# One written order for all engines from the last output product on, token transposes moved to TensorE, and conditional weight splits in smaller blocks

## The chip, the cores and the metric

The kernel runs on one core of a Trainium2 chip. The engines are TensorE (PE, with its weight loads shown apart as PEld), VectorE (DVE), ScalarE (ACT), GpSimd (POOL) and SyncE (SP, which here only issues DMAs). The metric is the device time of one execution in microseconds (us); a kernel's time is the median of its runs. Times within the kernel come from one profiled execution.

## The reference

Three layers follow each other. The queries, keys and values are 4 x 8 x 576 x 64 (batch, heads, sequence, head size); the attention is causal by blocks of 64.

```python
attn = softmax(mask(q @ k.T / sqrt(64))); x = attn @ v        # -> 2304 tokens x 512
xn = x / rms(x) * rms_g
x = (silu(xn @ w_gate) * (xn @ w_val)) @ w_out                # 512 -> 1536 -> 512
logits = normed(x) @ normed(expert_emb).T / tau               # 8 experts, tau = 0.1
e = argmax(logits); gate_w = softmax(logits)[e]
out = gate_w * (relu(x @ w1[e]) @ w2[e])                      # 512 -> 1024 -> 512, one expert a token
```

Which expert a token gets is found at run time, so the kernel routes: it sorts the tokens by expert in a table in DRAM, gathers 128 tokens of one expert at a time, and scatters the results to their rows.

## The kernel before, in words

**Tiles.** The 2304 tokens are nine units `u` of 256 tokens (`NU` = 9, the last is `NU-1`), each in two halves `j` of 128. For accuracy, most operands are a sum of two 16-bit parts, hi and lo, and a product is made as hi x hi + hi x lo + lo x hi, three matmuls where one would do.

**First layer of a unit.** `gate_mm` (L530) makes the gate product `g` and the value product `v` for one of six pieces `s` of the 1536 hidden columns: 2 x 24 products of 128 x 256 for `g` and the same for `v`. ACT takes the tanh (`gate_t`, L541), DVE combines (`gate_a`, L547 and L549), ACT writes the hi part of `hT` and POOL the lo part (`gate_b`, L554 and L555). `out_mm` (L567) then makes the output product of one half `j`, 36 products of 128 x 512, six for each piece of `hT`. `out_ev` (L578 to L591) brings the result into `R`, 128 tokens as hi and lo, one buffer. `R` is written to DRAM (`x2s`), and SP starts a DMA transpose of it into `x2T` (L590), from which PE makes the routing logits (`route_a`, L608). For the second half of the last unit, PE transposes `R` itself (L1103), and DVE copies the result out of the accumulator bank (L1104).

**Routing.** `route_b` to `route_d` find the expert of each token, its gate weight and its place, and POOL scatters rows into the table `tbl` (L672). While the last unit is still computed, `fullest` (L816 on) picks the two experts with most tokens so far and gathers the first table rows of the fullest into `tb2`; `fullest_ids` (L846) transposes `tb2` on PE (L849), DVE copies out the token numbers, POOL gathers the tokens of the first two steps (`xg`, L747), SP transposes them by DMA into `xt` (L749), and the expert's weights are loaded in four quarters a layer (`raw`, L722) and split into hi by ACT (`whi`, L727) and lo by DVE (`wlo`, L728).

**Expert steps.** There are 20 steps of 128 tokens: `mm1` (L764) is the first product, `ev1` the relu, `mm2` (L788) the second product, `ev2` the scaling and the scatter into the output (L796). Steps 0 and 1 use the expert found early. While they run, `T` counts the tokens of each expert; DVE makes `nbc`, the number of blocks (L1114 and L1115), a small product with `nbc` gives the order of all other steps (L1119), and POOL fetches the token numbers of steps 2 and 3 (L1127) and their tokens (L747 again). From step 2 on a step that has another expert than the step before loads new weights: `next_w` (L732 to L737) puts the split of a layer's four quarters into one conditional block on ACT and DVE.

**Order.** Up to the last output product the Tile scheduler orders the work, by priorities that the program sets (`step`) and by what is ready in its model. From `manual_schedule()` on (L1075) each engine runs its instructions as the program writes them. Before the change, that call stands behind the last output product; `seq` lists what stands ahead of it. Every engine runs its own queue in order, so a waiting instruction holds all behind it.

Of the kernel before, what the change touches and what calls it, by code (L numbers as in the profile page):

```python
# [8 lines left out]
F32 = mybir.dt.float32  # L9
F16 = mybir.dt.float16  # L10
# [8 lines left out]
P = 128  # L19
# [12 lines left out]
def attention_moe_moe(ctx: ExitStack, tc: tile.TileContext, q, k, v, w_gate, w_val, w_out, rms_g, emb, tau, w1, w2, out):  # L32
# [540 lines left out]
    def out_ev(u, j):  # L573
# [12 lines left out]
        if (u, j) == (NU - 1, 1):  # L586
            nc.scalar.dma_start(out=x2s[r0:r0 + P, :], in_=R)
            fl['R'] = R
            return
# [135 lines left out]
    def split_w(l, behind=()):  # L725
        for c in range(NC):
# [5 lines left out]
    def next_w(l, i):  # L732
# [3 lines left out]
        with tc.If(ch > 0):  # L736
            split_w(l)  # L737
# [4 lines left out]
    def gather(i, ids=None, last=UNIT):  # L742
# [5 lines left out]
        xt = xt_b[i % 3]  # L748
        tr = nc.sync.dma_start_transpose(out=xt, in_=xg)  # L749
        fl[f"xg{i}"], fl[f"xt{i}"] = ld.ins.name, tr.ins.name  # L750
        xgT[i] = xt
# [93 lines left out]

    def fullest_ids():  # L846
        t2 = ps_g.tile([P, 3, 2], F32, tag="o", name="t2", bufs=2)
        for c in range(3):
            tr = nc.tensor.transpose(t2[:, c, :], fl["tb"][0:2, :, c], idn[0:2, 0:2])  # L849
            tc.add_manual_dep(tr.ins, marks[-1], NOSYNC, reason="not before this product")  # L850
# [3 lines left out]
        for z in range(2):  # L854
            gather(z, id2[:, z:z + 1])
        fl["ev"] = [nc.values_load(em_i[0:1, z:z + 1], engines=[ENG.SP], min_val=0, max_val=NE - 1,
                                   skip_runtime_bounds_check_because="made on the chip in this range") for z in range(2)]
        for l in range(2):
            preload(0, l, ('no', 'tb_in')[l])
            split_w(l, ('gate_t', 'gate_a'))  # L860
# [108 lines left out]
    def step(kind, u, s):  # L969
        tc.cur_priority += PRI  # L970
        if kind == "gate":
# [5 lines left out]
            if u == NU - 1 and s == FS:  # L977
                fullest_ids()
# [6 lines left out]
        else:  # L985
            out_mm(u, s)
            if u == NU - 1 and s == 0:
                preload(1, 0, None)
            out_ev(u, s)
            if u == NU - 1 and s == 0:  # L990
                preload(1, 1, "x2T")
# [9 lines left out]
        if kind == "out" and s == 0 and u == NU - 1:  # L1001
            route(u, [0])
        if kind == "out" and s == 1 and u < NU - 1:
# [67 lines left out]
    seq += [("out", NU - 1, 0), ("out", NU - 1, 1)]  # L1071
# [3 lines left out]
    ctx.enter_context(tc.manual_schedule())  # L1075
    fin = late[0].tile([P, 16], F32, name="fin")
# [22 lines left out]
    u, js = NU - 1, [1]  # L1099
    mm1(0, range(3), behind=fl['out'])  # L1100
    xp = ps_g.tile([P, 2 * KD, P], F16, tag="o", name="xp", bufs=2)
    for c in range(2 * KD):
# [139 lines left out]
```

## Time and profile before

| what | value |
|---|---|
| median of 3 runs | 868.64 us (865.67 to 872.69) |
| the profiled execution | 876.56 us |
| its span on the chip | 874.8 us |
| its mean granted TensorE clock | 0.967 |
| PE busy | 795.9 us, 91% |
| DVE, ACT, POOL busy | 461.2, 450.0, 356.0 us |
| mean DMA rate | 154 GB/s |

The attention and most of the first layer fill the span up to about 600 us. The change starts in the last unit of the first layer, and the first expert products run at about 635 us. A timeline gives the start and the duration of an instruction, or of several alike in a row (`x24`), and in brackets how long its engine stood idle before it and what ended the wait. [...]

### The profile page before, as it was taken

What the parts mean: (1) busy time and instruction counts of PE and PEld (TensorE: products, weight loads), DVE (VectorE), ACT (ScalarE), POOL (GpSimd) and SP (SyncE); (2) the same over time, 40 slices, a digit from 0 to 9 for tenths busy, and PEclk for the clock granted to TensorE, in tenths of its full rate; (3) what the DMA queues carried; (4) which work ended last, traced back from release to release, by engine and by line L of the source; (5) the groups of instructions that cost most, each with busy time, mean ns of one, the idle gap of its engine ahead of it and who ended that gap; (6) DMA issues with size and microseconds to landing.
All of it is one profiled execution on the core that took longest, in us unless ns stands there. A gap on an engine that the chain in (4) does not pass through costs nothing. (4 is left out here: it accounts for less than half of the span.)

```text
span 874.8 us, 21909 instructions
## 1 busy us (share of the span) xinstructions
PE 795.9 (91%) x8574; PEld 602.6 (69%) x8574; DVE 461.2 (53%) x981; ACT 450.0 (51%) x929; POOL 356.0 (41%) x362
## 2 busy tenths in 40 slices
PE   2679799879999999989999999999988999999994
PEld 2579477757667777767777777758576777667771
DVE  6999978635355435355545454225542275462352
ACT  6978776845455656555746442212411274462351
POOL 5556466756533656543746322222323121202110
PEclk9989889989999999999999999999999999999997
DMA  8565899885777676687785351114755499998794
GB/s 240 163 191 141 182 246 208 163 152 100 123 151 139 117 137 113 119 159 140 133 134 104 64 105 23 28 45 113 226 158 124 85 291 298 208 320 190 181 238 128
DMA packets 296637, 135.11 MB, mean 154 GB/s; under 512 B 249852, under 2 KB 280743, under 8 KB 296522
## 3 DMA queue, kind: packets, MB, share of 16 engines
q1 hardware_dynamic: 288650, 117.00, 62.5%
q0 software_dynamic: 4080, 10.56, 4.3%
q10 hardware_dynamic: 3792, 6.03, 2.1%
q8 instruction: 70, 1.15, 0.6%
q14 instruction: 45, 0.37, 0.1%
HBM read 129.30 MB, written 10.25 MB: 160 GB/s over the span
## 5 line engine op out<-in xcount | busy, mean ns | idle before, releaser
L530 PE MATMUL g<-xT,wg 128*128 128x256 f16 x1296 | 158.5, 277 | 1.7 <-DMA xT<-hl 1.7
L530 PE MATMUL v<-xT,wv 128*128 128x256 f16 x1296 | 158.6, 277 | 0.0
L567 PE MATMUL o<-wo,hT 128*128 128x512 f16 x648 | 152.6, 384 | 3.2 <-ACT o L580 3.2
L530 PEld LDWEIGHTS <-wg 128*128 128x128 f16 x1296 | 126.7, 100 | 25.3 <-issue 2.0
L530 PEld LDWEIGHTS <-wv 128*128 128x128 f16 x1296 | 125.1, 99 | 16.3
L764 PE MATMUL h<-xt,whi 128*128 128x128 f16 x1280 | 112.1, 220 | 4.5 <-DMA xt<-xg 3.5
L764 PE MATMUL h<-xt,wlo 128*128 128x128 f16 x640 | 110.0, 220 | 0.7 <-issue 0.5
L567 PEld LDWEIGHTS <-hT 128*128 128x128 f16 x648 | 61.2, 98 | 67.8 <-issue 5.2
L764 PEld LDWEIGHTS <-whi 128*128 128x128 f16 x1280 | 99.9, 98 | 10.6 <-issue 6.2
L728 DVE SCALAR_TENSOR_TENSOR wlo<-raw,whi 128x1024 f16<-128x1024 f32 x64 | 76.7, 1236 | 48.0 <-ACT whi L727 43.4
L788 PE MATMUL o<-whi,hl 128*128 128x512 f16 x320 | 96.4, 383 | 2.4 <-issue 2.4
L555 POOL TENSOR_TENSOR hT<-h,hT 128x512 f16<-128x512 f32 x54 | 63.7, 1179 | 73.6 <-ACT hT L554 71.9
L417 POOL TENSOR_TENSOR pl<-pf,ph 128x512 f16<-128x512 f32 x66 | 69.6, 1076 | 52.7 <-issue 45.7
L788 PEld LDWEIGHTS <-hl 128*128 128x128 f16 x480 | 46.5, 99 | 57.1 <-issue 6.6
L727 ACT ACTIVATE whi<-raw 128x1024 f16<-128x1024 f32 x64 | 65.2, 1051 | 39.9 <-DMA raw<-in_moe_w_dram 29.2
L796 POOL DMA_INDIRECT out_dram<-ob,ido x18 | 20.1, 1116 | 158.6 <-ACTq L736 81.6
L353 DVE TENSOR_REDUCE nb<-sc 128x1 f32<-128x384 f32 (+3 forms) x88 | 54.0, 636 | 46.0 <-PE sc L321 40.0
L453 PE MATMUL av<-vT,ptl 128*128 128x64 f16 (+2 forms) x480 | 56.9, 197 | 22.4 <-DMA ptl<-pl 15.4
L453 PE MATMUL av<-vT,pth 128*128 128x64 f16 (+2 forms) x960 | 64.7, 197 | 10.3 <-DMA pth<-ph 8.9
L453 PEld LDWEIGHTS <-pth 128*128 128x128 f16 (+2 forms) x960 | 52.7, 104 | 21.2 <-DMA pth<-ph 11.1
L372 ACT ACTIVATE pf<-sc,nb 128x128 f32<-128x128 f32 (+3 forms) x128 | 66.0, 527 | 2.3 <-ACT nb L354 0.4
L453 PEld LDWEIGHTS <-ptl 128*128 128x128 f16 (+2 forms) x480 | 45.5, 104 | 27.3 <-DMA ptl<-pl 18.0
(226 smaller groups left out, 1295.3 us busy)
## 6 DMA issues: line engine op xcount, KB each, us to landing
raw<-in_moe_w_dram SPq DMA_DIRECT2D x172, 512.0 KB
st<-in_moe_w_out_dram SPq DMA_DIRECT2D x12, 512.0 KB
st<-in_moe_w_gate_dram SPq DMA_DIRECT2D x11, 512.0 KB
st<-in_moe_w_val_dram SPq DMA_DIRECT2D x11, 512.0 KB
x2s<-R ACTq DMA_DIRECT2D x18, 256.0 KB
nat<-in_k_dram SPq DMA_DIRECT2D x16, 256.0 KB
nat<-in_q_dram SPq DMA_DIRECT2D x16, 256.0 KB
nat<-in_v_dram SPq DMA_DIRECT2D x16, 256.0 KB
```

What stands on the lines that cost most here:

```text
L353: nc.vector.tensor_reduce(out=nb[:, z], in_=sc[:, 0:hpb * keys].rearrange("p (j k) -> p j k", k=keys), axis=AX.X, op=ALU.max)
L372: nc.scalar.activation(out=pf[:, j * keys:(j + 1) * keys], in_=scs[j // hpb][:, (j % hpb) * keys:(j % hpb + 1) * keys], func=ACTF.Exp, sca ...
L417: nc.gpsimd.tensor_tensor(out=pl[:, z:y], in0=pf[:, z:y], in1=ph[:, z:y], op=ALU.subtract)
L453: mm = nc.tensor.matmul(out=o, lhsT=x, rhs=w, start=first, stop=(h == H - 1 and kb == nkb - 1 and i == 2), skip_group_check=True)
L530: mm = nc.tensor.matmul(out=o[:, j, :], lhsT=w[cw][:, kt, f * P:(f + 1) * P], rhs=x[:, cx * KD + kt, :], start=(n == 0), stop=(n == 3 * KD ...
L555: nc.gpsimd.tensor_tensor(out=hT[1][fp], in0=h, in1=hT[0][fp], op=ALU.subtract)
L567: mm = nc.tensor.matmul(out=o, lhsT=hT[ch][f // 2][:, f % 2, j * P:(j + 1) * P], rhs=wo[cw][:, f, :], start=(f == 0 and n == 0), stop=(f = ...
L727: hi = nc.scalar.activation(out=whi[l][c], in_=raw[l][c], func=ACTF.Copy, scale=ES)
L728: lo = nc.vector.scalar_tensor_tensor(out=wlo[l][c], in0=raw[l][c], scalar=ES, in1=whi[l][c], op0=ALU.mult, op1=ALU.subtract)
L764: mm = nc.tensor.matmul(out=h[:, f, :], lhsT=w[:, kt, :], rhs=x[:, cx * KD + kt, :], start=(n == 0), stop=(n == 3 * KD - 1))
L788: nc.tensor.matmul(out=o, lhsT=x[:, cx, kt, :], rhs=w, start=(n == 0), stop=(n == 3 * K2 - 1))
L796: nc.gpsimd.indirect_dma_start(out=out, out_offset=bass.IndirectOffsetOnAxis(ap=(ido if ids is None else ids)[:, i:i + 1], axis=0), in_=ob ...
```

## The change

There are three parts.

1. The written order begins earlier: the two output products of the last unit leave `seq` and are written out, piece by piece, with the work of the other engines between the pieces. `fullest_ids` is cut in two: `fullest_w` (weight loads and splits) stays with the gates, and the rest (transposes of `tb2`, token gathers) stands behind piece 1 of the first output product. In the expert part, `route_p` and `route_d` go ahead of `fin` and `nbc`.
2. `turn` transposes 128 tokens with eight PE products and one DVE copy. It now also serves the first half of the last unit (instead of the DMA transpose into `x2T`) and the tokens of the third step, `xgT[2]` (instead of the DMA transpose into `xt`).
3. `next_w` makes two conditional blocks of two quarters each, where one block of four was.

```diff
-        if (u, j) == (NU - 1, 1):
+        if u == NU - 1:
             nc.scalar.dma_start(out=x2s[r0:r0 + P, :], in_=R)
             fl['R'] = R
             return
...
-    def split_w(l, behind=()):
-        for c in range(NC):
+    def split_w(l, behind=(), cs=range(NC)):
+        for c in cs:
...
         ch = val(1, i, [ENG.Activation, ENG.DVE], 1)
-        with tc.If(ch > 0):
-            split_w(l)
+        for z in range(0, NC, 2):
+            with tc.If(ch > 0):
+                split_w(l, cs=range(z, z + 2))
...
-    def gather(i, ids=None, last=UNIT):
+    def gather(i, ids=None, last=UNIT, pe=False):
...
-        xt = xt_b[i % 3]
-        tr = nc.sync.dma_start_transpose(out=xt, in_=xg)
-        fl[f"xg{i}"], fl[f"xt{i}"] = ld.ins.name, tr.ins.name
-        xgT[i] = xt
+        xgT[i] = xt_b[i % 3]
+        if not pe:
+            nc.sync.dma_start_transpose(out=xgT[i], in_=xg)
...
+    def fullest_w():
+        fl["ev"] = [nc.values_load(em_i[0:1, z:z + 1], engines=[ENG.SP], min_val=0, max_val=NE - 1,
+                                   skip_runtime_bounds_check_because="made on the chip in this range") for z in range(2)]
+        for l in range(2):
+            preload(0, l, ('no', 'tb_in')[l])
+            split_w(l, ('gate_t', 'gate_a'))
+
     def fullest_ids():
-        t2 = ps_g.tile([P, 3, 2], F32, tag="o", name="t2", bufs=2)
+        t2 = ps_g.tile([P, 3, 2], F32, tag="g", name="t2")
         for c in range(3):
-            tr = nc.tensor.transpose(t2[:, c, :], fl["tb"][0:2, :, c], idn[0:2, 0:2])
-            tc.add_manual_dep(tr.ins, marks[-1], NOSYNC, reason="not before this product")
+            nc.tensor.transpose(t2[:, c, :], fl["tb"][0:2, :, c], idn[0:2, 0:2])
...
-        fl["ev"] = [nc.values_load(em_i[0:1, z:z + 1], engines=[ENG.SP], min_val=0, max_val=NE - 1,
-                                   skip_runtime_bounds_check_because="made on the chip in this range") for z in range(2)]
-        for l in range(2):
-            preload(0, l, ('no', 'tb_in')[l])
-            split_w(l, ('gate_t', 'gate_a'))
...
             if u == NU - 1 and s == FS:
-                fullest_ids()
+                fullest_w()
...
             out_mm(u, s)
-            if u == NU - 1 and s == 0:
-                preload(1, 0, None)
             out_ev(u, s)
-            if u == NU - 1 and s == 0:
-                preload(1, 1, "x2T")
...
-        if kind == "out" and s == 0 and u == NU - 1:
-            route(u, [0])
...
-    seq += [("out", NU - 1, 0), ("out", NU - 1, 1)]
...
     ctx.enter_context(tc.manual_schedule())
+
+    def turn(dst, src, bank):
+        for c in range(2 * KD):
+            nc.tensor.transpose(bank[:, c, :], src[:, c * P:(c + 1) * P], idh)
+        nc.vector.tensor_copy(dst, bank)
+
+    u = NU - 1
+    for s in range(NFP):
+        out_mm(u, 0, s)
+        if s == 1:
+            fullest_ids()
+    preload(1, 0, None)
+    out_ev(u, 0)
+    preload(1, 1, None)
+    for s in range(NFP):
+        out_mm(u, 1, s)
+        if s == 1:
+            turn(x2T[u, 0], fl['R'], ps_g.tile([P, 2 * KD, P], F16, tag="v", name="xp"))
+        if s == 2:
+            route_a(u, [0])
+            route_b(u, [0])
+        if s == 4:
+            for f in (route_c, route_p, route_d):
+                f(u, [0])
+    out_ev(u, 1)
...
-    u, js = NU - 1, [1]
-    mm1(0, range(3), behind=fl['out'])
-    xp = ps_g.tile([P, 2 * KD, P], F16, tag="o", name="xp", bufs=2)
-    for c in range(2 * KD):
-        nc.tensor.transpose(xp[:, c, :], fl['R'][:, c * P:(c + 1) * P], idh)
-    nc.vector.tensor_copy(x2T[u, 1], xp)
+    js = [1]
+    mm1(0, range(3))
+    turn(x2T[u, 1], fl['R'], ps_g.tile([P, 2 * KD, P], F16, tag="o", name="xp", bufs=2))
...
+    route_c(u, js)
     nc.tensor.matmul(out=T[0:NE, 0:1], lhsT=ohs, rhs=ones[:, 0:1], start=True, stop=False)
     nc.tensor.matmul(out=T[0:NE, 0:1], lhsT=oh[:, 1, :], rhs=ones[:, 0:1], start=False, stop=True)
-    route_c(u, js)
+    route_p(u, js)
+    route_d(u, js)
     nc.vector.tensor_scalar(out=fin[0:NE, 0:1], in0=T[0:NE, 0:1], scalar1=0.5 * P - 0.5, scalar2=1.0 / P, op0=ALU.add, op1=ALU.mult)
     nc.vector.tensor_scalar(out=nbc[0:NE], in0=fin[0:NE, 0:1].to_broadcast([NE, P]), scalar1=ROUND, scalar2=-ROUND, op0=ALU.add, op1=ALU.add)
-    route_p(u, js)
-    route_d(u, js)
-    mm1(1, range(1))
+    mm1(1, range(2))
     nc.tensor.matmul(out=T[:, 1:], lhsT=nbc, rhs=ord_m, start=True, stop=True)
...
-        gather(2 + z, d23[:, z:z + 1], 0)
+        gather(2 + z, d23[:, z:z + 1], 0, not z)
...
     nc.vector.tensor_copy(gw, tp[:, 1, :])
+    turn(xgT[2], xg_b[2], h_b[0][:, 0:4, :].bitcast(F16).rearrange("p a (b c) -> p (a b) c", c=P))
```

The scheduler's part of the order changes too. On PE, the place is the end of the last unit's gates. `t<-idn,tb` is the transpose of `tb2`; numbers at the end of a name tell its buffers apart. Before:

```order
L530 LDWEIGHTS wg_190
L530 MATMUL g<-xT,wg_190 128x256
L849 MATMUL t_9591<-idn,tb_9283 128x2 x3
L530 LDWEIGHTS wv_191
L530 MATMUL v<-xT,wv_191 128x256
```

With the change:

```order
L530 LDWEIGHTS wv_192
L530 MATMUL v<-xT,wv_192 128x256
L856 MATMUL t_9636<-idn,tb_9283 128x2 x3
L567 LDWEIGHTS hT_2_197
L567 MATMUL o<-wo_193,hT_2_197 128x512
```

The transpose stood ahead of the last 24 gate products, and stands behind all of them now. The first 12 output products (pieces 0 and 1) went ahead of the last 128 gate products; the other 24 follow the transpose.

On ACT, the place is the end of the expert's weight split, while PE makes the last output products (`whi_3` is the last quarter of the second layer, `hT_5` the last piece of `hT`). The difference, with - for before and + for the change:

```order
 L727 ACTIVATE whi_1_9254<-raw_1_9250 128x1024
 L727 ACTIVATE whi_2_9255<-raw_2_9251 128x1024
+L727 ACTIVATE whi_3_9256<-raw_3_9252 128x1024
 L554 ACTIVATE hT_5_200<-h 128x512
-L727 ACTIVATE whi_3_9256<-raw_3_9252 128x1024
-L578 ACTIVATE R<-o 128x512
-L580 ACTIVATE o,rts<-o 128x512
-L591 DMA x2s<-R 128x1024
 L578 ACTIVATE R<-o 128x512
```

The last piece of `hT` is written behind all eight conversions, not behind seven of them.

On DVE, the place is the routing of the last 128 tokens, between the first products of step 1. With the change:

```order
L653 COPY pay<-place 128x1
L654 COPY pay<-tokid 128x1
L655 TENSOR_REDUCE rts<-l 128x1
L656 TENSOR_SCALAR rts<-rts 128x1
L657 RECIPROCAL pay<-rts 128x1
L665 TENSOR_TENSOR ohs<-ohs,oh 128x8
L666 TENSOR_TENSOR pos<-C,eb 128x8
L667 TENSOR_TENSOR pos<-pos,oh 128x8
L669 TENSOR_REDUCE rts<-pos 128x1
L670 CAST pi<-rts 128x1
L1132 TENSOR_SCALAR fin<-T 8x1
L1133 TENSOR_SCALAR nbc<-fin 8x128
```

Before, the last two rows (there L1114 and L1115) stood ahead of the ten others.

## Rows read from the trace of the kernel before

**Rows 1.** The page's top: span, busy times, DMA tenths by slice

```profile
span 874.8 us, 21909 instructions
...
PE 795.9 (91%) x8574; PEld 602.6 (69%) x8574; DVE 461.2 (53%) x981; ACT 450.0 (51%) x929; POOL 356.0 (41%) x362
...
DMA  8565899885777676687785351114755499998794
```

**Rows 2.** Timeline of PE: start, duration, operation, [idle before <- releaser]

```profile
605.57 2.78 PE L530 MATMUL g<-xT,wg 128*128 128x256 f16 x24
...
610.81 2.78 PE L530 MATMUL g<-xT,wg 128*128 128x256 f16 x24
615.25 0.50 PE L849 MATMUL t<-idn,tb 2*128 2x2 f32 x3 [1.65 <-DMA tb<-tbl,r]
615.68 4.46 PE L530 MATMUL v<-xT,wv 128*128 128x256 f16 x24
619.97 15.70 PE L567 MATMUL o<-wo,hT 128*128 128x512 f16 x72
...
640.13 1.06 PE L1103 MATMUL xp<-idh,R 128*128 128x128 f16 x8
```

**Rows 3.** Waits of PE, 530 to 870 us: total, times, longest

```profile
PE h L764 <- DMA xt<-xg: 3.5, 2, 2.3
...
PE L L608 <- DMA x2T<-R: 2.3, 2, 2.0
```

**Rows 4.** Windows: us, busy of five engines, PEclk, DMA share, GB/s

```profile
615.25:620.00 4.75, 4.75 (x28) 3.66 (x29) 0.89 (x4) 4.75 (x7) 3.13 (x3) 0.64 0.72 241
639.60:643.00 3.40, 3.40 (x36) 3.40 (x34) 2.58 (x15) 0.90 (x3) 0.57 (x1) 0.51 0.92 282
643.00:651.70 8.70, 8.52 (x156) 8.19 (x153) 6.09 (x38) 1.23 (x2) 2.04 (x2) 1.00 0.47 165
662.70:665.06 2.36, 0.08 (x1) 0.00 (x0) 0.00 (x0) 0.69 (x1) 1.01 (x1) 1.00 1.31 149
670.00:750.00 80.00, 80.00 (x940) 59.44 (x940) 37.59 (x32) 36.46 (x40) 13.95 (x12) 1.00 0.79 211
```

**Rows 5.** Timeline of ACT around the last output product

```profile
615.77 5.88 ACT L727 ACTIVATE whi<-raw 128x1024 f16<-128x1024 f32 x6
...
622.92 0.61 ACT L554 ACTIVATE hT<-h 128x512 f16<-128x512 f32 x1
624.78 1.06 ACT L727 ACTIVATE whi<-raw 128x1024 f16<-128x1024 f32 x1 [1.25 <-DMA raw<-in_moe_w_dram]
```

**Rows 6.** Timeline of POOL from 616 to 657 us

```profile
616.78 1.02 POOL L747 DMA_INDIRECT xg<-x2s,id  x1 [0.15 <-DVE t L547]
...
623.61 1.73 POOL L555 TENSOR_TENSOR hT<-h,hT 128x512 f16<-128x512 f32 x1 [4.56 <-ACT hT L554]
...
656.72 0.96 POOL L747 DMA_INDIRECT xg<-x2s,d  x1 [0.64 <-issue]
```

**Rows 7.** Timeline of DVE from 620 to 648 us

```profile
620.84 10.13 DVE L728 SCALAR_TENSOR_TENSOR wlo<-raw,whi 128x1024 f16<-128x1024 f32 x8
...
639.25 0.69 DVE L579 SCALAR_TENSOR_TENSOR R<-o,R 128x512 f16<-128x512 f32 x1 [4.71 <-ACT R L578]
...
641.23 0.69 DVE L1104 COPY x2T<-xp 128x1024 f16<-128x1024 f16 x1 [0.22 <-PE xp L1103]
...
646.76 0.13 DVE L653 COPY pay<-place 128x1 f32<-128x1 f32 x1
...
647.97 0.15 DVE L670 CAST pi<-rts 128x1 int32<-128x1 f32 x1
```

**Rows 8.** Timeline of SP, issuing the transposes of tokens

```profile
660.01 3.79 SPq L749 DMA_TRANSPOSE xt<-xg  x2
```

**Rows 9.** Line L736, the conditional block; and DVE behind one

```profile
L736 DVEq COMPARE_BRANCH  x51: 43/50/72, 661.9 to 856.4; - x51
...
746.58 1.23 DVE L775 SCALAR_TENSOR_TENSOR hl<-h,hl 128x1024 f16<-128x1024 f32 x1 [0.55 <-ACTq L736]
```

More of the change, by code (lines that the diff above doesn't have):

```diff
@@ L1000, in step @@
             gate_b(u + 1, 0)
-        if kind == "out" and s == 0 and u == NU - 1:
-            route(u, [0])
-        if kind == "out" and s == 1 and u < NU - 1:
+        if kind == "out" and s == 1:
             route(u, [0, 1])
@@ L1135, in attention_moe_moe @@
     nc.vector.tensor_tensor(out=ri, in0=em[:, 56:57], in1=m_row, op=ALU.add)
-    mm1(1, range(1, K2))
+    mm1(1, range(2, K2))
     ld = nc.gpsimd.indirect_dma_start(out=tb.rearrange("p a b -> p (a b)"), out_offset=None, in_=tbl,
```

## The prediction, made before the changed kernel ran

> **What bounds the kernel now.** I read the page's top first, then the waits of TensorE (PE), then the order of time on each engine around the longest of them. PE is busy for 795.9 of 874.8 us [rows 1], so a change can only gain where PE waits or runs slowly. Three waits in the stretch that the change touches are over 1 us: 1.65 us for `tb2`, the table rows of the fullest expert, transposed in `fullest_ids` [rows 2], 2.0 us for the DMA transpose of the last unit's first tokens (`x2T`; the longest of that row's two), and 2.3 us for the DMA transpose of the third step's tokens (`xt`, the longest of two) [rows 3]. Two of the three cost more than themselves. [...] The 24 products behind the first wait took 4.46 us, against 2.78 for 24 like them at full clock [rows 2]: 1.7 us. The 3.40 us at 0.51 cost 3.4 x 0.49 = 1.7 us. In the middle of the expert steps, 670 to 750, PE computes 80.00 of 80.00 us [rows 4]; later there is one more wait for `xt`, 3.5 - 2.3 = 1.2 us [rows 3].
>
> **The change, part by part**, on the clock of the profiled execution. One product of the output layer takes 15.70 / 72 = 0.218 us, and 24 gate products (610.81 - 605.57) / 2 = 2.62 us from start to start [rows 2].
>
> *The tb2 wait.* Twelve output products of the last unit (pieces 0 and 1, whose inputs are long there) now go before the remaining gate products, and the transposes of `tb2` come after all gates. Before, PE had done the gates ahead of them at 615.25 - 1.65 = 613.6 and went on at 615.25, when the rows were there [rows 2]; now it gets there at 613.6 + 12 x 0.218 + 2.62 = 618.8, 3.6 us after they landed. The wait goes, -1.65, and with it the slow stretch, -1.7. What hides it is the gate work of the last piece.
>
> *What is late next: the last piece of `hT`.* The output of the first tokens has 24 products left at 619.3; after 18 of them, at 619.3 + 18 x 0.218 = 623.2, it needs piece 5. ScalarE (ACT) now writes that piece behind all eight conversions of the expert's weights; before, one of the eight stood behind it. Six conversions took 5.88 us, 0.98 each [rows 5]. They start when the last tanh is done, about 616.9 (gates end 2.62 later than before), so the eighth starts at 616.9 + 7 x 0.98 = 623.8 and ends at 624.8, if its quarter of the weights has landed. That is the open point: before, the eighth waited 1.25 us for that DMA, until 624.78 [rows 5]. Between the transfers then lay two token gathers, issued at 616.78 and after [rows 6]; now these are issued only after 620.9, since DVE takes their addresses behind the first conversion (the conversions began at 620.84 in the trace) [rows 7]. So the quarter should land sooner; the bounds are 623.8 and 624.78, and I take the first because the gathers are out of its way. Then `hT` hi is there at 624.8 + 0.6 = 625.5, and PE waits 2.3 us. Its lo part comes from POOL: 1.73 us in the row that ran beside the same DVE work [rows 6], so 627.3, while PE has 0.43 us of work in between: 1.4 us more, less some overlap, 1.3. Sum +3.6 (3.0 to 4.7). Behind a wait of that size I take one slow stretch like the two of [rows 4], +1.7; the lower bound is 0, as after the 2.3 us for `xt`.
>
> *The x2T wait.* PE transposes the tokens itself, out of `R`, with six output products between that and the routing product, 1.3 us, against a copy of 0.69 us [rows 7]. The wait goes, -2.0 [rows 3], and its slow stretch, -1.7. ACT, which could overwrite `R` only when the DMA transpose had read it, no longer waits for that; that is no time of PE's, it starts the routing of the last tokens earlier. [...]
>
> *The order on DVE.* The operand `nbc` of the next small product is made behind ten routing instructions instead of ahead of them: 646.76 to 648.1, 1.35 us later [rows 7], while PE meets that product 12 expert products later, 12 x 8.52/156 = 0.66 us [rows 4]. Bounds 0 and +0.9; I take +0.4.
>
> *The third step's tokens.* Before, the gather was issued at 656.72, its DMA transpose at 660.01 [rows 6, 8], and PE started at 665.06 [rows 4], 5.05 us after. Now PE does it when its queue reaches it. `R` of the last tokens is complete about 638.4 (before, its last part began at 639.25) [rows 7], and 20.8 us lay between that row and 660.01; with 0.9 for the DVE order the tokens are there at 660.1, and PE comes for them at about 661. So -2.3, plus 8 transposes, +0.53, plus what nothing covers: a copy of 0.69 us [rows 7] and two handoffs, +0.9 (0.8 to 1.4). [...]
>
> *The conditional splits.* 37 blocks become 74 on ACT and DVE. A branch takes 50 ns on DVE, and the longest that an instruction of the next work was held by one I could read is 0.55 us [rows 9]. So 37 more cost 2 to 20 us on engines that are idle half of the time, and PE gets both results a whole product phase later. On PE's path I take 0. Finer blocks could at best take away the 1.2 us of the later wait for `xt` [rows 3], whose loads stand behind such blocks; consecutive changes of expert, in which DVE is full, could lose as much.
>
> **Sum:** -1.65 - 1.7 + 3.6 + 1.7 - 2.0 - 1.7 + 0.53 + 0.4 - 2.3 + 0.53 + 0.9 = **-1.7 us**. The profiled execution took 876.56 us, 7.9 above the median of the three runs, 868.64; the terms are waits and work of PE, so I take them off the median: **866.9 us**. Its own bounds: 3.0, no slow stretch, 0 on DVE and 0.8 at the copy give -4.5; 4.7 and 0.9 on DVE give -0.1, say 0.
>
> **The rivals.**
> 1. *The last piece of `hT` costs next to nothing* (weights land early, no slow stretch, half the wait): -1.7 - 1.7 - 1.8 = -5.2, 863.4 us. For it: the transfers are alone on the queues. Against: ACT's order. With the -1.2 above it is 862.2.
> 2. *Slower: that piece becomes the bound.* If the eighth quarter lands at 626 or later, the wait is 4.8 or more, and PE, which already lost one slow stretch, gets a second one from the lo part: -1.7 + 1.2 + 1.7 = +1.2, and with the upper ends on DVE and at the copy +2.2, 870.8 us. It decides from a landing of about 625.5 on, where the term alone eats the gain. For it: ACT did wait for this DMA before.
> 3. *Given back.* DMA engines are at 9 tenths or more in the slices of the expert steps [rows 1]; if transfers bound them, PE comes earlier and waits longer at the next one: 0, 868.6 us. Against: only 1.2 us of such waiting shows [rows 3], and the loads start when PE frees the weights, so they move with it.
> 4. *The transposes slow the clock.* 8 transposes and 0.9 us without work, just before the third step: a slow stretch there, +1.7, makes the whole 0, 868.6 us. Against: the 2.36 us there before ended at clock 1.00 [rows 4]. [...] No row shows transposes alone at full clock: the eight of [rows 2] fell in a stretch that was slow already.
>
> **How the numbers follow.** Forecast 0.48 (its own range 864.1 to 868.6), rival 1 0.17, rival 2 0.15, rivals 3 and 4 0.10 each. One per cent, 8.7 us, is about what a measurement here can tell from no change; the three runs lie 7.0 us apart. All cases lie within it, so: faster 0.06, within 0.90, slower 0.04. The cases reach from rival 1's better end, 862.2, to rival 2, 870.8; a median of three such runs can itself lie a microsecond off, so the range is 861.2 to 871.8.
>
> **What would show it.** Right: no PE wait on `tb2`, `x2T` or `xt` before the third step; a wait of 2 to 4 us at the output product for `hT` piece 5, ended by ACT and then POOL, with a clock of about 0.5 behind it; a wait of about 0.9 us on the copy into `xt`. Wrong: that piece there on time, or the eighth conversion still waiting for its DMA beyond 625; a slow clock in the third step; waits on `raw` or `xt` growing between 690 and 850; any sizeable wait of PE that ACT's or DVE's branches end.

## The result and the profile after

The changed kernel took **878.64 us** (median of four runs, 877.85 to 879.93), the kernel before 868.54 us in this comparison (four runs, 865.67 to 872.69): ratio 1.0114, 95% interval 1.0071 to 1.0157. The forecast was 866.9 us, range 861.2 to 871.8: wrong in its size, and in its sign. Repeated twice, on two chips and with more runs, the same kernel came out at 1.0019 (0.9982 to 1.0055, not clear of zero) and 1.0055 (1.0022 to 1.0089). Single executions scatter: 31 of the kernel before, in one set, lie between 867.15 and 884.24 us, so four against four can miss by several (and three of the four runs of before are those known ahead of the prediction). The repeats give a loss of 1.7 and 4.8 us, the profiles below some 4.5; the rest of the first difference is not explained here. Medians are of all runs of a set, ratios are taken from its fast runs alone.

The page after has PE as busy as before, over a span 1.2 us longer [rows 1]; the profiled execution of the kernel before took 876.56 us, 8 above its median, so this pair shows little of the 10.1 us:

```profile
span 876.0 us, 22094 instructions
...
PE 795.9 (91%) x8590; PEld 603.2 (69%) x8590; DVE 465.7 (53%) x983; ACT 449.9 (51%) x929; POOL 357.1 (41%) x362
```

The waits of PE from the last unit's end on (total, times, longest):

```profile
PE o L788 <- issue: 3.8, 1, 3.8
PE o L567 <- ACT hT L554: 1.7, 1, 1.7
PE o L788 <- ACT whi L727: 1.7, 1, 1.7
PE xp L1073 <- ACT R L578: 1.5, 1, 1.5
PE o L567 <- POOL hT L555: 1.0, 1, 1.0
PE h L764 <- DVE xt L1074: 0.8, 1, 0.8
PE h L764 <- DMA xt<-xg: 0.6, 1, 0.6
...
PE L L608 <- DMA x2T<-R: 0.4, 1, 0.4
...
```

The wait for `tb2` is gone, that of `x2T` [rows 3] is down to 0.4 us, and at the third step 0.8 us for the copy stand where 2.3 for `xt` did (the 0.6 for `xt` lie at a later step). Three kinds stand in their place: `hT` (forecast), `R` at the transposes of the second tokens, and the last product, `mm2` of step 19, twice, where the kernel before has one wait of 2.4 us. In order of time on PE, with what ended each wait:

```profile
618.21 2.78 PE L530 MATMUL v<-xT,wv 128*128 128x256 f16 x24
620.92 0.50 PE L856 MATMUL t<-idn,tb 2*128 2x2 f32 x3
621.35 4.06 PE L567 MATMUL o<-wo,hT 128*128 128x512 f16 x18
627.16 0.60 PE L567 MATMUL o<-wo,hT 128*128 128x512 f16 x2 [1.74 <-ACT hT L554]
628.71 5.31 PE L567 MATMUL o<-wo,hT 128*128 128x512 f16 x16 [0.95 <-POOL hT L555]
633.86 0.61 PE L1073 MATMUL xp<-idh,R 128*128 128x128 f16 x8
...
643.46 0.40 PE L1073 MATMUL xp<-idh,R 128*128 128x128 f16 x4 [1.55 <-ACT R L578]
644.18 0.40 PE L1073 MATMUL xp<-idh,R 128*128 128x128 f16 x4 [0.33 <-DVE R L579]
...
664.73 0.61 PE L1073 MATMUL h<-idh,xg 128*128 128x128 f16 x8
666.12 0.27 PE L764 MATMUL h<-xt,whi 128*128 128x128 f16 x2 [0.78 <-DVE xt L1074]
```

The transposes of `tb2` (620.92) no longer wait, and the 24 gate products ahead of them take 2.78 us, not 4.46 [rows 2]. Behind `hT` the granted clock was 0.50 of full speed for one stretch of 3.41 us, as forecast (the columns are those of [rows 4]):

```profile
629.20:632.61 3.41, 3.41 (x10) 1.22 (x9) 3.41 (x4) 0.60 (x1) 0.00 (x0) 0.50 0.77 159
```

One profiled execution of each kernel says little where each scatters by itself. From the timelines of all profiles of either order I took three stretches: from the last unit's first gate product to step 2, from there to step 19, and from step 19 to the end (a step starts with its first product on PE).

| profiles | gates to step 2 | step 2 to 19 | step 19 to the end |
|---|---|---|---|
| before (first, and run again) | 97.1, 93.1 | 179.7, 180.0 | 30.0, 32.1 |
| before, splits in two blocks | 96.3 | 180.5 | 29.0 |
| before, code moved (b_pad) | 93.7 | 178.8 | 32.8 |
| changed (first, and run twice again) | 96.1, 96.2, 98.1 | 177.1, 178.9, 183.1 | 32.8, 33.0, 33.2 |
| changed, one block | 96.3 | 178.2 | 34.1 |
| changed, code moved (a_pad) | 98.1 | 179.7 | 29.6 |

The first column is 1.9 us more for the changed order in the mean (five profiles against four, of which those of before lie 4 us apart), the second the same within its scatter, the third 2.9 more (without the two kernels whose code was moved). That is a loss of some 4.5 us, at the upper end of what the repeats measured. The forecast had -1.7 in the first column and nothing in the third.

### The profile page after: what moved, and what is told of

It is laid out like the page before. It is cut to its first block, busy times and chain, and to the rows that moved or that the text cites. A ratio compares the mean times of both kernels' runs of the same rounds, so it can differ in the third digit from the quotient of the medians.

```text
span 876.0 us, 22094 instructions
## 1 busy us (share of the span) xinstructions
PE 795.9 (91%) x8590; PEld 603.2 (69%) x8590; DVE 465.7 (53%) x983; ACT 449.9 (51%) x929; POOL 357.1 (41%) x362
## 3 DMA queue, kind: packets, MB, share of 16 engines
q8 instruction: 70, 1.15, 0.6%
## 5 line engine op out<-in xcount | busy, mean ns | idle before, releaser
L567 PE MATMUL o<-wo,hT 128*128 128x512 f16 x648 | 154.6, 386 | 5.4 <-ACT o L580 2.7
L530 PE MATMUL v<-xT,wv 128*128 128x256 f16 x1296 | 156.7, 275 | 0.0
L764 PE MATMUL h<-xt,whi 128*128 128x128 f16 x1280 | 110.0, 219 | 1.4 <-DVE xt L1074 0.8
L453 PEld LDWEIGHTS <-ptl 128*128 128x128 f16 (+2 forms) x480 | 46.1, 105 | 30.1 <-DMA ptl<-pl 21.0
```

What stands on the lines that cost most here:

```text
L453: mm = nc.tensor.matmul(out=o, lhsT=x, rhs=w, start=first, stop=(h == H - 1 and kb == nkb - 1 and i == 2), skip_group_check=True)
L530: mm = nc.tensor.matmul(out=o[:, j, :], lhsT=w[cw][:, kt, f * P:(f + 1) * P], rhs=x[:, cx * KD + kt, :], start=(n == 0), stop=(n == 3 * KD ...
L567: mm = nc.tensor.matmul(out=o, lhsT=hT[ch][f // 2][:, f % 2, j * P:(j + 1) * P], rhs=wo[cw][:, f, :], start=(f == 0 and n == 0), stop=(f = ...
L764: mm = nc.tensor.matmul(out=h[:, f, :], lhsT=w[:, kt, :], rhs=x[:, cx * KD + kt, :], start=(n == 0), stop=(n == 3 * KD - 1))
```

## Experiments

**Is the difference in the changed code, and do the splits cost?** `b_same` and `a_same` are the two kernels unchanged. `a_one_block` undoes the third part of the change alone, `b_two_blocks` does it alone:

```diff
-        for z in range(0, NC, 2):
-            with tc.If(ch > 0):
-                split_w(l, cs=range(z, z + 2))
+        with tc.If(ch > 0):
+            split_w(l)
```

Expected of `b_same`: 

> The kernel before, unchanged, to get a profile of an execution near its median. The profile shown of it took 876.56 us, 8 above the median of its runs, and the profile after took 877.85, at its own median; so in this pair of traces only 1.2 us of the 10.1 us are seen. Theory A (the difference lies ahead of the changed code): a profile of an execution at 866 to 870 us reaches the last unit's gates (568.0 us in the profile before, 570.0 after) 6 to 9 us sooner, at 559 to 562, and the rest lasts as long as before. Theory B (the difference lies in the changed part): the gates of the last unit start at 567 to 569 again and the stretch from there to the end is 6 to 9 us shorter than the 306.8 us of the profile before. Ratio 1.000 within 0.004.

Expected of `a_same`: 

> The changed kernel, unchanged, for a second profile and for the spread. Theory A: 877 to 880 us, with the last unit's gates at 569 to 572 us, and a stretch from there to the end of 306 us. Theory B: the stretch from there to the end varies or is longer than 306 us in this second profile.

Expected of `a_one_block`: 

> The changed kernel with the old next_w (one conditional block of four quarters), all else as changed. Theory C (the 37 added blocks cost the time, on ACT and DVE or by code that has to be fetched): back to 867 to 870 us. Theory A or B without a part of the blocks: 877 to 880 us, within 1 us of the changed kernel. My forecast put the blocks at 0.

Expected of `b_two_blocks`: 

> The kernel before with the conditional split in two blocks of two quarters alone. Theory C: 876 to 880 us. If the blocks are not the cause: 866 to 871 us, as before.

Measured: medians 872.50, 877.37, 877.60 and 874.93 us, beside 874.54 for the kernel before (31 runs, 867.15 to 884.24); ratios 0.998 (0.9945 to 1.0015), 1.0019 (0.9982 to 1.0055), 1.0024 (0.999 to 1.0058) and 1.0001 (0.9964 to 1.0038). Theory C falls from both sides: the blocks cost nothing that shows. Each ratio leaves room for some 3 us either way. Theory A falls too: the last unit's gates start at 565.8 to 570.0 us in these profiles of both kernels, without an order between them, and the instruction lists of the two kernels are the same on every engine up to there. (The execution of 866 to 870 us that the theory asked for was not caught: the profiled one of `b_same` took 876.10.) What lies ahead of the change does add to the scatter: in three profiles of the changed kernel the gates start at 570.0, 565.8 and 564.3 us. Theory B stays, without its size.

**Why the end is longer.** The program runs 20 steps; the last product is reached by a taken branch past the code of steps that are not executed. These kernels add PE products to step 24, which never runs, so what is executed stays the same and only the place of the tail's code moves (`a_pad` with 12; `b_pad` the same edit on the kernel before, with 16):

```diff
         gather(i + 2, last=0)
+        if i == NSTEP - 1:
+            for _ in range(12):
+                nc.tensor.matmul(out=h_b[i % 2][:, 0, :], lhsT=idh, rhs=idh, start=True, stop=True)
         mm1(i)
```

Expected of `a_pad`: 

> The changed kernel with 12 PE products more in the code of step 24, which is never executed (20 steps run): nothing that is executed differs, only where the code of the last product lies. Theory D (the last product, reached by a taken branch, now starts just ahead of the end of a fetched piece of PE's code, so PE stalls for its code twice, 1.7 and 3.5 to 3.9 us, where the kernel before stalls once, 2.4 or 3.9): the stall after three products goes, one of 2 to 4 us stays; from the start of step 19 to the end 30 to 31 us instead of 33; 2 to 3 us less than the changed kernel's 877.4, about 874.5 to 875.5. Rival E (the stall comes from DMA traffic or chance at the tail): two stalls as before, 33 us, 877 to 878.

Expected of `b_pad`: 

> The kernel before with 16 PE products more in the never executed step 24, that is, with as many PE instructions more ahead of the last product as the change's 16 transposes make. Theory D: it gets the changed kernel's stalls, one of about 1.7 before the last product and one of 3.5 to 3.9 after its third matmul; 33 us from step 19 to the end instead of 29 to 32; 1 to 3 us slower than before, 876 to 877.5. Rival E: one stall, 874.5.

The starts of the last product on PE, after, with the waits in front of them:

```profile
855.64 0.59 PE L788 MATMUL o<-whi,hl 128*128 128x512 f16 x2 [1.74 <-ACT whi L727]
...
860.30 1.03 PE L788 MATMUL o<-whi,hl 128*128 128x512 f16 x2 [3.85 <-issue]
```

The same of the kernel before, in its first profile and run again (`b_same`), then `a_pad`, then `b_pad`:

```profile
857.85 0.79 PE L788 MATMUL o<-whi,hl 128*128 128x512 f16 x2 [2.40 <-issue]
```

```profile
856.76 1.01 PE L788 MATMUL o<-whi,hl 128*128 128x512 f16 x2 [3.86 <-issue]
```

```profile
857.51 0.59 PE L788 MATMUL o<-whi,hl 128*128 128x512 f16 x2 [2.37 <-issue]
```

```profile
852.38 0.59 PE L788 MATMUL o<-whi,hl 128*128 128x512 f16 x2 [1.36 <-ACT whi L727]
...
856.72 1.01 PE L788 MATMUL o<-whi,hl 128*128 128x512 f16 x2 [3.52 <-issue]
```

Moving the code swaps the pattern: the changed kernel gets the single stall, the kernel before the double one, whose second part comes after three products in all of them. The other profiles of this document agree. Nine are of kernels whose PE code ahead of the tail is, like the changed kernel's, 16 products longer than before: all have the second stall, 2.8 to 4.1 us, and take 32.7 to 34.1 us from step 19 to the end. Eight are of kernels with none, 20 or 28 more: none has it, and they take 28.3 to 32.1. (The first stall is put down to ACT, whose last conversion was done at 854.8 in the changed kernel; PE began 0.8 us later.) Transfers that the trace marks as instructions, on the queue where they have 16384 bytes each, began at 850.41, 853.10 and 857.72 us in the changed kernel; PE starts 1.5 us behind the end of the second (854.14), and goes on 1.6 us behind that of the third (858.70). In all 17 profiles PE comes out of each of these stalls, 26 in number, 1.2 to 1.7 us after the end of such a transfer. The granted clock of the same window was 0.77 in the changed kernel, 0.97 in `a_pad` and 0.77 in `b_same`:

```profile
853.00:868.00 15.00, 8.59 (x29) 3.01 (x26) 2.95 (x3) 2.96 (x4) 1.00 (x1) 0.77 0.48 156
```

```profile
853.00:868.00 15.00, 7.48 (x34) 3.12 (x32) 4.14 (x4) 3.96 (x5) 1.98 (x2) 0.97 0.53 170
```

```profile
853.00:868.00 15.00, 8.23 (x24) 3.00 (x24) 2.02 (x2) 2.20 (x3) 2.00 (x2) 0.77 0.52 164
```

It was as low in `b_same`, behind a single stall of 3.86 us, as in the changed kernel: the single stall differs from profile to profile (1.1 to 3.9 us), and what sets its length is open. From step 19 to the end, `a_pad` took 29.6 us and `b_pad` 32.8, as theory D said; the two profiles of the unchanged kernel before took 30.0 and 32.1, so the move is worth 1 to 3 us. In the times it does not stand out: `a_pad` was expected at 874.5 to 875.5 us and took 876.43, `b_pad` 877.88, beside 874.31 for the kernel before; ratios 1.003 (0.9988 to 1.0072) and 1.0026 (0.9985 to 1.0067); 2 to 3 us are at the edge of what ten runs tell. The 16 transposes of the change, 32 PE instructions with their weight loads, are what moved the code.

**What holds `R`.** ACT, in the changed kernel:

```profile
626.49 0.61 ACT L554 ACTIVATE hT<-h 128x512 f16<-128x512 f32 x1
630.19 0.60 ACT L578 ACTIVATE R<-o 128x512 f16<-128x512 f32 x1 [3.09 <-PE o L567]
632.64 0.58 ACT L580 ACTIVATE o<-o 128x512 f32<-128x512 f32 x1 [1.86 <-DVE R L579]
...
635.91 0.33 ACTq L587 DMA_DIRECT2D x2s<-R  x1
...
642.81 0.60 ACT L578 ACTIVATE R<-o 128x512 f16<-128x512 f32 x1 [5.13 <-DMA x2s<-R]
```

And SP:

```profile
632.34 5.09 SPq L722 DMA_DIRECT2D raw<-in_moe_w_dram  x8
```

`R` is complete at 632.6, but its write to `x2s` is issued at 635.91, 3.3 us later, and lands at 642.8, when ACT may write the second tokens into `R` (5.13 us of waiting). SP had issued eight loads of the second expert's weights from 632.34 on. In the instruction list, the write and the first of these loads name the same DMA counter, and the write comes later in it:

```
L722 DMA raw_0_9237<-in_moe_w_dram 128x4x256 [waits DMAHW6_49,DVE_49]
L587 DMA x2s<-R 128x1024 [waits DMAHW6_49,Activation_49]
```

So it waits for a load that it has nothing to do with: that load's last part landed at 635.84, 0.07 us ahead of the write's issue. Then it shares the DMA engines with the other seven: from 635.91 to 642.81 us these were busy for a share of 1.00, at 338 GB/s. The write's other wait, for ACT itself, was over at 633.3. In all six profiles with this order of loads and write, the write is issued 3.5 to 3.8 us behind the first load. Before, four of the eight loads waited for `x2T`. `a_r_first` puts the write first:

```diff
-    preload(1, 0, None)
     out_ev(u, 0)
+    preload(1, 0, "x2s")      # waits for the write of R
     preload(1, 1, None)
```

Expected of `a_r_first`: 

> The changed kernel with the write of R (the last unit's first tokens, one buffer) put ahead of the eight loads of the second expert's weights, which now wait for it. Theory F (the write, which stood behind those loads, holds R, so ACT writes the second tokens 5 us late and PE waits 1.9 to 2.3 us at their transposes): ACT's wait of 5.1 us for the write goes, PE's wait at the transposes of R falls under 0.5, and the stretch from the last unit's gates to step 3 is 1.5 to 2.3 us shorter (102.0 to 104.1 in the changed kernel). Time 875 to 876. Rival: the wait is taken over by the next one (the routing of the second tokens, nbc or the token gathers), and step 2 starts as late as now; 877.4.

ACT and PE in it:

```profile
629.71 0.58 ACT L580 ACTIVATE o<-o 128x512 f32<-128x512 f32 x1 [1.41 <-DVE R L579]
629.72 0.33 ACTq L587 DMA_DIRECT2D x2s<-R  x1
...
636.75 0.60 ACT L578 ACTIVATE R<-o 128x512 f16<-128x512 f32 x1 [2.27 <-PE o L567]
```

```profile
638.56 0.61 PE L1073 MATMUL xp<-idh,R 128*128 128x128 f16 x8
```

The write is issued as soon as `R` is complete, ACT waits only for PE's product, and the transposes of the second tokens wait for nothing. From step 0 to step 1, where the wait for `R` lies, it took 6.3 us, against 8.5 to 11.0 in the five profiles of the changed order. Gates to step 2 took 93.6 us, against 96.1 to 98.1; to step 3, the stretch that the expectation names, 101.6 against 102.0 to 105.9. Theory F holds in the profile. The time, 876.70 us, ratio 1.0013 (0.9976 to 1.0051), is 0.7 us under the changed kernel's on another chip (877.37), inside the scatter.

**The last piece of `hT`.** `a_hT_first` puts it ahead of the second layer's conversions:

```diff
-            split_w(l, ('gate_t', 'gate_a'))
+        split_w(0, ('gate_t', 'gate_a'))
...
     out_ev(u, 0)
+    split_w(1)
```

It also puts the two token gathers behind hT's lo part on POOL.

Expected of `a_hT_first`: 

> The changed kernel with the last piece of hT ahead of the second layer's weight conversions on ACT (these follow the last unit's first result) and ahead of the token gathers on POOL. My forecast's term: the waits of 1.7 for hT hi and 1.0 for hT lo go, and the slow stretch behind them (3.4 us at half clock) with them: 2.7 + 1.7 = 4.4 us less up to the end of the last output product. Rival: the work behind it is not ready either (R, whose write still stands behind loads; DVE, which has four conversions more ahead of the tokens' copy), so that 2 us or more come back as waits at the transposes of R or at route; then only 1 to 2.5 us are left at step 2. Time 873 to 876.5.

Measured: 878.15 us, ratio 1.0049 (0.9997 to 1.01). Its waits between the gates and step 3:

```profile
PE L L608 <- DVE x2T L1076: 4.0, 1, 4.0
...
```

`hT` is gone from the list, and 4.0 us stand at the logits: DVE had four conversions ahead of the copy. Gates to step 2 took 95.6 us. The rival holds. `a_hT2` leaves the conversions ahead of `R`, and moves the first tokens' transposes behind piece 3 of the second product, and their routing into the first expert product; `a_best2` is that with the two mends above:

Expected of `a_hT2`: 

> The changed kernel with the last piece of hT ahead of conversions 5 to 8 on ACT and of the token gathers on POOL, as in the run before, but with the conversions left ahead of R on DVE; the transposes of the first tokens go behind piece 3 of the second output product, their logits behind that product, and the rest of their routing into the first expert product. Theory: hT's waits (1.7 to 2.1 and 0.6 to 1.0) and the slow stretch behind them go and nothing takes their place but R's write behind the loads, which is left as it is (a wait of 1.5 to 2.5 at the second tokens' transposes). Step 2 starts 3 to 4.5 us sooner after the last unit's gates than in the changed kernel (96.2 to 98.1 there). Rival: DVE, whose eight conversions end at the same time as now, holds the first tokens, and the wait reappears at their transposes or logits; under 2 us gained.

Expected of `a_best2`: 

> All three mends in one: the last piece of hT first (as in a_hT2), the write of R ahead of the second expert's loads, and 12 products in the never executed step 24, which move the last product's code. Theory: 4.4 (hT and its slow stretch) + 2 (R) + 3 (code) = up to 9 us less than the changed kernel, 5 to 7 less than the kernel before: ratio 0.992 to 0.995. No wait of PE over 1 us between the gates and step 3 but the copy into xt (0.8). Rival: the routing of both token halves on DVE is the next bound, and 2 us come back before step 2: ratio 0.995 to 0.998.

Measured: `a_hT2` 877.21 us, 1.0024 (0.9993 to 1.0056); `a_best2` 872.87 us, 0.9982 (0.9954 to 1.0011), where 0.992 to 0.995 was expected and 0.995 to 0.998 by its rival. Gates to step 2 took 96.4 and 94.6 us. The wait moved on once more, in `a_best2`:

```profile
PE C L644 <- DVE oh L636: 3.1, 2, 2.5
...
PE xp L1077 <- DVE R L579: 0.6, 1, 0.6
...
```

**The whole again, and the third step's tokens.** `a_same2` is the changed kernel again, beside the same runs of the kernel before. `a_dma_xt` undoes `turn` for `xgT[2]`, with eight products in step 24 so that the tail's code lies as in the changed kernel:

```diff
-        gather(2 + z, d23[:, z:z + 1], 0, not z)
+        gather(2 + z, d23[:, z:z + 1], 0)
...
-    turn(xgT[2], xg_b[2], h_b[0][:, 0:4, :].bitcast(F16).rearrange("p a (b c) -> p (a b) c", c=P))
```

Expected of `a_same2`: 

> The changed kernel once more, for the size of the whole effect. The first comparison gave +10.1 us from four runs of each kernel; the second +0.2% (-0.2 to +0.55). From the profiles so far I expect +3 us: about +1 between the last unit's gates and step 3, -1 in the steps, +2.8 in the tail. Ratio 1.002 to 1.005. If the first comparison was right, 1.011.

Expected of `a_dma_xt`: 

> The changed kernel with the third step's tokens transposed by DMA again, as before the change, and eight products in the never executed step 24 in place of the eight transposes, so that the code of the tail lies as in the changed kernel. My forecast's terms: the wait for xt comes back (1.2 to 2.3 us), the transposes (0.5) and the copy's wait (0.8) go; 0.5 to 1.4 us slower than the changed kernel between step 1 and step 2 (17.90 us there in four profiles, 17.8 to 19.2 before). Rival: the DMA transpose is ready as PE comes, since PE arrives later than before: 1.3 us faster.

Measured: 880.61 us, 1.0055 (1.0022 to 1.0089), and 877.37 us, 1.0048 (1.0009 to 1.0088). PE at the start of step 2 in `a_dma_xt`, where no wait stands in front of the first product:

```profile
658.65 0.38 PE L788 MATMUL o<-wlo,hl 128*128 128x512 f16 x1
658.87 0.28 PE L764 MATMUL h<-xt,whi 128*128 128x128 f16 x2
```

From step 1 to step 2 it took 16.51 us, and 17.90 in each of five profiles of the changed order: 0.61 of transposes and 0.78 of waiting for the copy make the 1.39. My expectation for this run had the wrong sign; its rival holds. The time does not show it: the ratio is near that of `a_same2`. The gather, on POOL, says why. After, then `a_dma_xt`:

```profile
657.25 0.96 POOL L748 DMA_INDIRECT xg<-x2s,d  x1 [0.65 <-DVE d L1162]
```

```profile
651.39 0.96 POOL L748 DMA_INDIRECT xg<-x2s,d  x1 [0.66 <-issue]
```

Step 1 starts at 648.22 and 642.36 there, so the gather is issued 9.03 us behind it in both. Before, it was 656.72 [rows 6] less 645.87: 10.85. So the tokens were 1.8 us earlier, by PE's steps; my reading is that PE had been held up by `R` while the routing of the first tokens went on, which no run shows by itself. The DMA transpose was quicker too: issued at 654.65 in `a_dma_xt`, it was done when PE came 4.2 us later, where 5.05 passed before.

**Do these three losses make the distance?** `a_three` undoes them: the write of `R` first, the third step's tokens by DMA, 12 products in step 24 (the edits above). `a_four` also puts `hT` first on ACT and POOL, with `R`'s lo part ahead of the last two conversions on DVE, and `a_four_pe` is `a_four` with the third step's transposes on PE:

```diff
+        split_w(1, ('hi', 'gate_a'), range(2))             # hi: behind the last piece of hT
+        split_w(1, ('hi', 'gate_a'), range(2, NC), "h")    # hi alone
...
     out_ev(u, 0)
+    split_w(1, (), range(2, NC), "l")                      # their lo parts behind R
```

Expected of `a_three`: 

> The changed kernel with the three losses undone: R's write ahead of the second expert's loads, the third step's tokens transposed by DMA, 12 products in the never executed step 24. If these three are the distance: gates to step 2 in 92 to 93 us (96.1 to 98.1 in the changed kernel, 93.1 to 97.1 before), tail 28 to 30 us, and in all 2 to 4 us faster than the kernel before, ratio 0.995 to 0.998, as my forecast had it (-1.7 us). If something else is at work: ratio 1.000 or above.

Expected of `a_four`: 

> a_three with the last piece of hT ahead of conversions 5 to 8 on ACT and of the token gathers on POOL, R's lo part ahead of the last two lo conversions on DVE, and the first tokens' logits behind piece 3. If hT is a fourth loss of its own: PE has no wait at hT, under 1 us at R and at the logits, and gates to step 2 takes 3 to 4 us less than in a_three; ratio 0.990 to 0.995. If the work of DVE is what bounds this stretch: waits of 2 us or more at the logits, at C or at the second tokens, and within 1.5 us of a_three.

Expected of `a_four_pe`: 

> a_four with the third step's transposes on PE, as in the change. From a_dma_xt (16.51 us from step 1 to step 2 by DMA, 17.90 by PE): 1.0 to 1.4 us slower than a_four. If the DMA transpose is late again in a_four, since PE comes earlier there: no difference, or 1 us faster.

Measured, beside 871.50 us for the kernel before: `a_three` **867.78 us, 0.9961 (0.9937 to 0.9986)**, faster than the kernel before (the changed kernel was not in this set; it had 1.0019 to 1.0114 in the others); `a_four` 870.34 us, 0.9999 (0.9974 to 1.0025); `a_four_pe` 868.75 us, 0.998 (0.9954 to 1.0005). The waits of `a_three` between the gates and step 3:

```profile
PE o L567 <- ACT hT L554: 1.9, 1, 1.9
PE h L764 <- DMA xt<-xg: 1.6, 1, 1.6
PE o L567 <- POOL hT L555: 0.8, 1, 0.8
PE L L608 <- DMA x2T<-R: 0.5, 1, 0.5
```

The time is where it was expected, the way there only in part. The tail took 30.1 us, with one stall of 2.7, and step 0 to step 1 6.3. But gates to step 2 took 94.4 us, not 92 to 93, since PE, no longer held at `R`, came early enough to wait for `xt` again, 1.6 us there. With the write of `R` alone put first it was 93.6 (`a_r_first`): from step 1 to step 2 PE's transposes cost 17.9 us there, the DMA 18.3 here. So two of the three are losses that come back in `a_three`, `R` and the tail; the third is none once `R` is mended. The same waits of `a_four`, and of `a_four_pe`:

```profile
PE h L773 <- DMA xt<-xg: 3.2, 1, 3.2
PE C L644 <- DVE oh L636: 1.0, 1, 1.0
PE xp L1084 <- DVE R L579: 0.9, 1, 0.9
```

```profile
PE C L644 <- DVE oh L636: 1.0, 1, 1.0
...
PE h L773 <- DVE xt L1085: 0.8, 1, 0.8
```

With `hT` mended, PE comes earlier still and waits 3.2 us for the DMA transpose; on PE the same tokens cost a wait of 0.8 and the transposes, and step 1 to step 2 takes 18.1 us, not 20.1. The expectation for `a_four_pe` (1.0 to 1.4 us slower) missed, and the case that it named beside it came true, by 2 us in the profiles. So whether `turn` pays at the third step hangs on when PE arrives. `hT`'s wait is no fourth loss that could be had back at this price: `a_four_pe` has the shortest stretch of all, 91.5 us, and is no faster than `a_three` by its times. Nor is `a_four`, expected 3 to 4 us ahead of `a_three` in that stretch: it took 93.5. Whether `a_four_pe` would be faster with more runs stays open.

## Why the prediction was wrong

Split by the starts of the steps, the forecast's terms and the means of the profiles (five of the changed order against four; in the tail as above) compare so:

| stretch | terms of the forecast | forecast | measured |
|---|---|---|---|
| gates to step 0 | `tb2`, `hT`, first tokens' transposes | +2.5 | +2.4 |
| step 0 to 1 | `x2T` and its slow stretch | -3.7 | 0.0 |
| step 1 to 2 | order on DVE, third step's tokens | -0.5 | -0.5 |
| step 2 to 19 | splits | 0 | -0.3 |
| step 19 to the end | none | 0 | +2.9 |

The forecast of -1.7 us missed in two places: the `x2T` term, whose gain did not come, and the tail, which had no term. The kernel before takes 7.8 to 12.3 us from step 0 to 1 in its four profiles, so the means are good to about 1 us there.

- **tb2**: right. The wait is gone in each profile of the changed order, and in the changed kernel's first the slow stretch too: the granted clock was 1.00 from 618.21 to 621.35 us.
- **hT**: right in place and mechanism, ACT and then POOL, with one slow stretch behind (3.41 us at a granted clock of 0.50); 1.7 + 1.0 us where I had 3.6. So that its stretch came out within 0.1 us of the forecast is in part luck. The DMA of the eighth quarter, which I called the open point, was not waited for, so rival 2 had no ground.
- **x2T**: the step that failed. The wait went as forecast, but -3.7 us (2.0 of waiting, and 1.7 for the 3.40 us at a granted clock of 0.51 behind it [rows 4]) took for granted that nothing is late next. I said that the change frees ACT from its wait for `R`, and put `R` of the last tokens complete at 638.4, with no working shown. It was complete at 644.1, in a trace 2.0 us later at the gates, and at 638.1 in `a_r_first` (there 0.8 earlier). ACT still waits, 5.1 us, now for `R`'s own write, which stands behind the loads of the second expert's weights. I had moved those loads ahead in my reading (they no longer wait for `x2T`) without asking which queue and which counter the write would meet. It costs PE 1.5 to 2.5 + 0.3 us, and in two of the five profiles, the two with 98.1 us in the table, one more slow stretch behind it (from 642.0 us in `a_pad`, from 639.2 in `a_same2`). With the write first, step 0 to 1 takes 6.3 us; the forecast's is 10.4 of the profile before less 3.7, so 6.7.
- **The order on DVE**: no wait for `nbc` shows; +0.4 was too much. The upper bound of 0.9 does not follow either: 1.35 - 0.66 is 0.7.
- **Third step's tokens**: the term was -0.9 (-2.3 + 0.5 + 0.9), and against the kernel before the size agrees: 0.6 of transposes and 0.8 of waiting where 2.3 of waiting were. But the new way of transposing is not what took the wait away. In the changed kernel the DMA would have been in time, and the transposes on PE cost 1.4 us more than it; I took the wait of before over into a kernel in which PE comes later. With `R` mended the wait is back, and the transposes save 0.4 us (`a_r_first` against `a_three`, one profile each). The 0.53 us for eight transposes, twice in the sum, is shown by no run; eight took 0.61 us at a granted clock of 1.00 (at 633.86 and at 664.73 in the changed kernel), 1.06 at 0.50 [rows 2].
- **The splits**: 0, right from both sides, within some 3 us.
- **The tail**: no term at all. The 16 transposes moved the code of the last product so that PE stalls twice there: +2.9 us in the mean of the profiles, 1.9 against the two profiles of the unchanged kernel before. The trace of before had the stall, 2.4 us in front of the last product, and I did not ask what sets it.
- **Given back** (rival 3): DMA engines at nine tenths or more is too much for the row: 5 of its 11 slices from 634 us on have a 9 [rows 1]. The changed kernel's first profile shows no growing waits on `xt` from step 2 on (0.6 us, once).
- **The slow clock from transposes** (rival 4): did not come. Eight transposes took 0.61 us at 664.73, just in front of the third step, and the granted clock was 1.00 from there to that step's first product at 666.12.

Together: -1.7 + 3.7 (what took the place of the `x2T` gain) + 2.9 (tail) - 0.4 (the other stretches) = +4.5 us, near the upper of the two repeats (0.55% of 875 is 4.8). The 10.1 us of the first comparison lie above that by more than I can account for; the range failed by these two, the missing terms and a scatter between sets of runs that I put at one microsecond, where sets of the same kernel before have medians from 868.5 to 875.3. Of the mended kernels only `a_three`, with `R` and the tail mended together, is clear of the kernel before by its times; each of the two alone is shown by the profiles.

## What to carry to other kernels

When loads are let go earlier, list every transfer that is issued behind them, a small write above all: here it waited 3.3 us for their counter and landed 6.9 us after its issue, and the buffer that it read was held as long (5.13 us of ACT's waiting). Price the removal of a wait in the kernel as changed, not as it was: whoever is delayed elsewhere finds the data ready, and whoever is no longer delayed waits again. And where a branch is taken near the end of a program, ask whether its target's place in the code is part of the time (1 to 3 us here); padding code that never runs tests that without touching anything executed.

## What the runs showed of the hardware

- One queue moved what the profile marks as instructions in transfers of 16384 bytes (70 of them, 1.15 MB, in the kernel before and in the changed one), and PE left each stall at the last product 1.2 to 1.7 us behind the end of one (17 profiles). With 16 products more ahead of it in the code, PE stalled again after three products, for 2.8 to 4.1 us (nine profiles); with none, 20 or 28 more it did not (eight).
- Two DMAs, issued by SP and by ACT, were tied by one counter, which the program gave both: a write whose data were ready at 632.6 was issued at 635.91, 0.07 us behind the last part of a load (635.84).
- Eight transposes on PE of 128 x 128 took 0.61 us between products at a granted clock of 1.00; it stayed at 1.00 from 632.64 to 857.90 us of the changed kernel's profile, where all 24 of the change's `turn` fall.
- Sets of runs of one and the same kernel had medians from 868.5 to 875.3 us in different sets, on several chips; ten runs against thirty left an interval of about 0.35% to either side.
